# Ordering the third batch's first transforms nearer to their use in a fused Fourier mixer and channel mix kernel

## Chip, cores and metric

One core of one Trainium2 chip. The metric is the device time of one execution in microseconds (us); lower is better. A difference counts as faster or slower from 2% on, which is 12 us here.

## The reference, cut to what matters

```python
def _attn_ref(x, w_r, w_i, b_r, b_i):          # x: 8 x 3072 x 256
    X = np.fft.rfft(x, axis=1)
    Yr = Xr @ w_r - Xi @ w_i + b_r
    Yi = Xr @ w_i + Xi @ w_r + b_i
    # soft shrink of Yr and Yi by 0.01
    return np.fft.irfft(Y, n=x.shape[1], axis=1)

def _moe_ref(x, mu_k, mu_r, w_k, w_v, w_r):    # on the result of the first
    xk = mu_k * x + (1.0 - mu_k) * x_prev      # x_prev: one place earlier in the sequence
    xr = mu_r * x + (1.0 - mu_r) * x_prev
    k = np.maximum(xk @ w_k, 0.0)
    return 1.0 / (1.0 + np.exp(-(xr @ w_r))) * (k * k @ w_v)
```

## The kernel before

The transform of 3072 points is done as 96 by 32, in matmuls. Per batch there are: **first** transforms (eight units, line 280; the first two batches do this step another way), whose result A goes to DRAM (Adr) and comes back in another layout; **second** transforms (line 378 for the first group, line 395 for the rest), **mixing** with the complex weights (line 423), **back** transforms (line 462), whose result V goes through DRAM too (Vdr), and **last** inverse transforms (line 543) that write YT. Then each of the batch's six tiles of tokens has four **key** units (line 635), one **receptance** unit (line 662) and two **value** units (line 679).

The kernel text holds a small scheduler. Each unit has a due time and needs; among the units that are ready by the scheduler's own estimate, the one with the earliest due time is written next into the program. So the due times decide the order, once, when the program is built; on the chip each engine follows that order.

```python
    READ_US, WRITE_US = 7.0, 5.0

    def first(b, t0, t1):
                ...
                def store(k):
                    nc.sync.dma_start(out=Adr[b][:, 8 * q:8 * q + 8, :], in_=a)
                    done["a", b, q] = k + WRITE_US
                    n = 4 * b + q + 4
                    if 8 <= n < 4 * B:
                        load_x(n // 4, n % 4)
                        done["x", n // 4, n % 4] = k + 9.0
                    if q == 3:
                        at(k + WRITE_US, fetch)

                def fetch(k):
                    for hf in range(2):
                        A2[b, hf] = a2_pool.tile([128, NG // 2, D], BF16, name="A2")
                        for cj in range(4):
                            r0 = 24 * cj + 12 * hf
                            nc.sync.dma_start(out=A2[b, hf][32 * cj:32 * cj + 32],
                                              in_=Adr[b][r0:r0 + 12].rearrange("g n d -> n g d"))
                        for u in range(3 * hf, 3 * hf + 3):
                            done["A2", b, u] = k + READ_US * (1 + hf) / 2
            ...
            return Unit(t0 + (t1 - t0) * (2 * q + p) / 8, 0.44, needs, issue)   # due time first
    ...
    P = 71.5
    START = 50.0
    for b in range(B):
        s = START + P * (b - 1)
        ...
        else:
            fb += first(b, s - 0.9 * P, s - 0.2 * P)
            fa += middle(b, s, s + 0.5 * P)
            fc += last(b, s + 0.75 * P, s + 0.95 * P)
```

Batches count from 0 in the text, so `b == 2` is the third.

## Time and profile before

| | before |
|---|---|
| time, median of 3 | 595.51 us (595.29 to 595.68) |
| profiled span | 593.3 us |
| TensorE busy | 566.7 us, 96% |
| VectorE busy | 519.3 us, 88% |
| ScalarE busy | 425.5 us, 72% |
| third batch's last first-transform starts | 93.96 us |
| its A (first half) back | 110.4 us |
| its second transform starts | 120.91 us |

A kernel like this is read from its bound engine: where does TensorE stand still, and what was it waiting for? The prediction shows the lines. The column that names "idle before" in the groups, and the list of waits, give the answer per stretch of time.

### The profile page before, as it was taken

What the parts mean: (1) busy time and instruction counts of PE and PEld (TensorE: products, weight loads), DVE (VectorE), ACT (ScalarE), POOL (GpSimd) and SP (SyncE); (2) the same over time, 40 slices, a digit from 0 to 9 for tenths busy, and PEclk for the clock granted to TensorE, in tenths of its full rate; (3) what the DMA queues carried; (4) which work ended last, traced back from release to release, by engine and by line L of the source; (5) the groups of instructions that cost most, each with busy time, mean ns of one, the idle gap of its engine ahead of it and who ended that gap; (6) DMA issues with size and microseconds to landing.
All of it is one profiled execution on the core that took longest, in us unless ns stands there. A gap on an engine that the chain in (4) does not pass through costs nothing.

```text
span 593.3 us, 12315 instructions
## 1 busy us (share of the span) xinstructions
PE 566.7 (96%) x4824; PEld 428.9 (72%) x4891; DVE 519.3 (88%) x834; ACT 425.5 (72%) x467; POOL 23.5 (4%) x53
## 2 busy tenths in 40 slices
PE   4989999999999999999999999999999999999996
PEld 3878666777767787677777777677876787776665
DVE  7788999789998899888998989988999889979883
ACT  6887967677768677676777677777776867766652
POOL 7001000000000000000000000000000000000000
PEclk9999999999999999999999999999999999999999
DMA  8936888624599256773478655683338722362223
GB/s 150 167 80 158 186 193 226 178 72 104 129 225 237 60 139 140 204 225 67 116 167 245 154 120 129 165 238 106 100 93 235 178 55 73 103 164 72 68 57 90
DMA packets 68878, 84.06 MB, mean 142 GB/s; under 512 B 9042, under 2 KB 53844, under 8 KB 68820
## 3 DMA queue, kind: packets, MB, share of 16 engines
q1 hardware_dynamic: 62916, 68.98, 41.7%
q0 software_dynamic: 5712, 14.03, 15.1%
q8 instruction: 38, 0.62, 0.4%
q10 hardware_dynamic: 192, 0.26, 0.2%
q14 instruction: 20, 0.16, 0.1%
HBM read 50.07 MB, written 47.19 MB: 164 GB/s over the span
## 4 chain that ended last, share of the span: by engine, by line
PE 81%; ACT 7%; DVE 4%; DMA 3%; issue 2%; SPq 1%; POOL 0%; POOLq 0%; DVEq 0%; ACTq 0%
PE banks L679 27%; PE banks L635 23%; PE banks L423 14%; PE banks L662 5%; PE banks L462 3%; PE banks L280 3%; PE banks L395 3%; ACT rl L641 2%; PE banks L543 2%; ACT rg L667 1%; DMA xs<-in_x_dram 1%; DMA Adr<-A 1%; ACT YT L227 1%; PE banks L353 1%; SPq L305 1%
## 5 line engine op out<-in xcount | busy, mean ns | idle before, releaser
L641 ACT ACTIVATE rl<-banks 128x1024 bf16<-128x1024 f32 x192 | 193.5, 1028 | 94.0 <-PE banks L635 88.2
L635 PE MATMUL banks<-xk,wk 128*128 128x512 bf16 x701 | 188.7, 379 | 5.3 <-DVE xk L608 0.7
L679 PE MATMUL banks<-wv,k 128*128 128x256 bf16 x1536 | 183.0, 272 | 0.4 <-ACT rl L641 0.3
L679 PEld LDWEIGHTS <-k 128*128 128x128 bf16 x1536 | 149.3, 98 | 29.1 <-issue 1.4
L647 DVE TENSOR_TENSOR k<-rl 128x1024 bf16<-128x1024 bf16 x192 | 130.3, 684 | 13.3 <-ACT rl L641 13.3
L635 PEld LDWEIGHTS <-wk 128*128 128x128 bf16 x768 | 73.9, 98 | 60.7 <-issue 3.1
L423 PEld LDWEIGHTS <-XT 128*128 128x128 bf16 x768 | 74.5, 98 | 16.4 <-issue 0.9
L423 PE MATMUL banks<-wr,XT 128*128 128x256 bf16 x384 | 73.3, 272 | 0.6 <-ACT A L227 0.2
L423 PE MATMUL banks<-wi,XT 128*128 128x256 bf16 x384 | 73.3, 273 | 0.0
L608 DVE SCALAR_TENSOR_TENSOR xk<-diff,muk,YT 128x512 bf16<-128x512 bf16 x96 | 69.1, 744 | 0.2
L608 DVE SCALAR_TENSOR_TENSOR xr<-diff,mur,YT 128x512 bf16<-128x512 bf16 x96 | 68.7, 744 | 0.0
L690 DVE TENSOR_TENSOR o<-banks,rg 128x1024 f32<-128x1024 f32 (+1 forms) x49 | 58.6, 1196 | 3.7 <-PE banks L679 3.4
L227 ACT ACTIVATE YT<-banks 128x768 bf16<-128x768 f32 x59 | 44.9, 827 | 12.1 <-PE banks L543 9.1
L662 PE MATMUL banks<-wrm,xr 128*128 128x256 bf16 x384 | 49.8, 272 | 0.1
L227 ACT ACTIVATE XT<-banks 128x1024 bf16<-128x1024 f32 (+2 forms) x45 | 42.8, 956 | 9.2 <-PE banks L395 8.4
L667 ACT ACTIVATE rg<-banks 128x1024 bf16<-128x1024 f32 x48 | 49.1, 1024 | 0.0
L227 ACT ACTIVATE A<-banks 96x1024 bf16<-96x1024 f32 (+1 forms) x41 | 41.3, 1022 | 8.0 <-PE banks L280 6.2
L440 ACT ACTIVATE z<-banks 128x1024 bf16<-128x1024 f32 x32 | 32.7, 1022 | 19.9 <-PE banks L423 19.8
L662 PEld LDWEIGHTS <-xr 128*128 128x128 bf16 x384 | 37.2, 98 | 11.6 <-issue 0.2
L227 ACT ACTIVATE V<-banks 128x1024 bf16<-128x1024 f32 x35 | 35.9, 1024 | 11.6 <-PE banks L462 10.6
L602 DVE TENSOR_TENSOR diff<-YT 128x1024 bf16<-128x1024 bf16 x48 | 32.8, 683 | 3.8 <-ACT YT L227 3.8
L452 DVE TENSOR_TENSOR Y<-z,Y 128x1024 bf16<-128x1024 bf16 x48 | 33.2, 693 | 1.7
(101 smaller groups left out, 437.1 us busy)
## 6 DMA issues: line engine op xcount, KB each, us to landing
out_dram<-o SPq DMA_DIRECT2D x188, 128.0 KB, 2.3
xs<-in_x_dram POOLq DMA_DIRECT2D x32, 384.0 KB, 6.2
Vdr<-V SPq DMA_DIRECT2D x192, 64.0 KB, 1.8
V<-Vdr SPq DMA_DIRECT2D x32, 384.0 KB, 6.3
Adr<-A SPq DMA_DIRECT2D x24, 384.0 KB, 5.3
A<-Adr SPq DMA_DIRECT2D x48, 192.0 KB, 4.5
wk<-in_moe_w_k_dram POOLq DMA_DIRECT2D x1, 512.0 KB, 11.7
wv<-in_moe_w_v_dram POOLq DMA_DIRECT2D x1, 512.0 KB, 13.5
```

The source lines that it names most:

```text
L227: nc.scalar.activation(out, in_, AF.Copy, bias=0.0, scale=1.0)
L423: nc.tensor.matmul(o, lhs, w[:, c, :], start=(w is wr and c == 0), stop=(w is wi and c == NCD - 1))
L452: nc.vector.tensor_tensor(out=y, in0=z, in1=y, op=ALU.subtract)
L602: nc.vector.tensor_tensor(out=df, in0=y, in1=yp, op=ALU.subtract)
L608: nc.vector.scalar_tensor_tensor(out=m[:, c, :], in0=df[:, c, :], scalar=mu[:, c:c + 1], in1=yp[:, c, :], op0=ALU.mult, op1=ALU.add)
L635: nc.tensor.matmul(ps[:, 512 * f:512 * f + 512], wk[:, c, 128 * ff:128 * ff + 128], xk[:, c, :], start=(c == 0), stop=(c == NCD - 1))
L641: nc.scalar.activation(rl, ps, AF.Relu, bias=0.0, scale=1.0)
L647: nc.vector.tensor_tensor(out=k2, in0=rl, in1=rl, op=ALU.mult)
L662: nc.tensor.matmul(ps[:, 256 * q:256 * q + 256], xr[:, c, 128 * q:128 * q + 128], wrm[:, c, :], start=(c == 0), stop=(c == NCD - 1))
L667: nc.scalar.activation(rg, ps, AF.Sigmoid, bias=0.0, scale=1.0)
L679: nc.tensor.matmul(ps[:, 256 * q:256 * q + 256], K2[t][:, ff, 128 * q:128 * q + 128], wv[:, ff, :], start=(ff == 0), stop=(ff == NCF - 1))
L690: nc.vector.tensor_tensor(out=o[:, lo:hi], in0=ps[:, lo:hi], in1=rg[:, lo:hi], op=ALU.mult)
```

## The change

The due times of the third batch's first transforms start later (121.5 - 0.5 x 71.5 = 85.75 us instead of 57.15) and end later (114.35 instead of 107.2). The intent is to do them nearer to their use and to let the second batch's work go ahead of them.

```diff
-            fb += first(b, s - 0.9 * P, s - 0.2 * P)
+            fb += first(b, s - (0.5 if b == 2 else 0.9) * P, s - (0.1 if b == 2 else 0.2) * P)
```

The order on TensorE that comes of it differs in one stretch only. Here F is a first-transform unit of the third batch, L a last inverse unit of the second batch, K, R and V the token units, S0 and S second transforms of the third batch, M mixing (half a unit). Both rows begin with the sixth F.

```
before: F F F V K V K R K K L V K V K L R L L K V L K L L V K L K R K         S0 S K V S K M V M F K S R M M ...
after:  F L L V K V K R K F K L L V K V K R K F L K V L L K V L K R K K V     S0 S S K V F M M K S R M M ...
```

## The prediction

> **What bounds the kernel now.** I read the page first: shares of the span by engine, then the chain that ended last.
>
> ```profile
> span 593.3 us, 12315 instructions
> ...
> PE 566.7 (96%) x4824; PEld 428.9 (72%) x4891; DVE 519.3 (88%) x834; ACT 425.5 (72%) x467; POOL 23.5 (4%) x53
> ...
> PEclk9999999999999999999999999999999999999999
> ...
> PE 81%; ACT 7%; DVE 4%; DMA 3%; issue 2%; SPq 1%; POOL 0%; POOLq 0%; DVEq 0%; ACTq 0%
> ```
>
> TensorE is busy for 96% of the span at full granted clock, and 81% of the last-ending chain is its matmuls. It runs one fixed order of work, so what matters is TensorE time that is lost while the instruction at its head waits. A change that only reorders cannot shorten its 566.7 us; it can only remove or add idle time. So I asked next for the busy time of each engine in the stretches around the third batch's first transforms (columns: stretch and length, then busy time and instructions of each engine, clock, DMA share, GB/s):
>
> ```profile
> 80.00:93.09 13.09, 12.98 (x91) 8.95 (x91) 12.14 (x18) 8.04 (x9) 0.00 (x0) 1.00 0.83 232
> 93.09:102.33 9.24, 9.19 (x62) 6.19 (x62) 8.49 (x12) 6.61 (x8) 1.01 (x2) 1.00 0.99 223
> 102.33:120.90 18.57, 17.73 (x170) 13.38 (x172) 14.71 (x26) 12.70 (x16) 0.00 (x0) 1.00 0.57 147
> 120.90:131.00 10.10, 9.96 (x87) 7.63 (x87) 8.85 (x15) 6.87 (x8) 0.00 (x0) 1.00 0.25 65
> ```
>
> From 93.09 to 131.00 us TensorE loses 0.05 + 0.84 + 0.14 = 1.03 us. That is nearly all that a better order could win here. The waits of TensorE from 93 to 121 us name part of it:
>
> ```profile
> PE banks L635 <- DVE YT L563: 0.4, 1, 0.4
> PE banks L543 <- ACT YT L227: 0.2, 1, 0.2
> ```
>
> Both belong to the second batch's last inverse transforms (line 543) and the padding behind them, which in this order come in a bunch just before their result is needed.
>
> Last I read the DMA queue of SyncE in order of time, because the third batch's first transforms go out to DRAM (Adr) and come back in another layout (A) before the second transform (line 378, the first of its kind for the batch) may start:
>
> ```profile
> 95.05 1.57 SPq L291 DMA_DIRECT2D Adr<-A  x2
> ...
> 104.61 3.90 SPq L305 DMA_DIRECT2D A<-Adr  x8
> 108.61 5.33 SPq L701 DMA_DIRECT2D out_dram<-o  x8
> ```
>
> The second of the two stores is issued at 96.30 us, the fetch at 104.61 (8.3 us for a store's round), and the four DMAs of the first half land by 110.4. The second transform starts at 120.91: **about 10 us of slack**, with nothing waiting.
>
> **What the Trainium skill says.** "DMA: Bandwidth & Descriptors", section "Two DMAs through the same engine are not ordered": a DMA that reads what another wrote must wait at the issuing engine for the first one's completion. The trace agrees: the queue stands still from the store to the fetch, and the landing of the fetches is one more trip. The same page, section "Issuing engines are not separate DMA queues": transfers of all issuing engines share the same 16 DMA engines and interleave. The trace agrees: the line of stores to Adr shows landings of 2.9 us at least, 5.3 median and 8.9 at most, the longest where loads of x and V are in flight beside them. "TensorE: Matmul & The Clock Gate", section "Measured speedup vs the span model": matmuls start and end strictly in the program's order. So a late A would stop everything behind it on TensorE; the trace of before has no late A and cannot show it, but its matmuls stand in the listed order.
>
> **The change part by part.** It adds and removes no matmul: the listing of the order has the same 9784 TensorE rows, with the same counts of each kind. Only the due times of the third batch's eight first-transform units move, and the scheduler gives a new order only from about 93.5 us to about 128 us; after that all engines' orders are equal again. Three effects.
>
> (1) *Where the transforms land.* Before, units start at 71.53 (three), 76.11, 84.84 and 93.09 (three). In the new order the first six stay where they are; the seventh and eighth go behind inverse transforms and token units. I placed them by adding the measured pace of the units in the new order, from 93.09: a first-transform unit 0.43 us (two matmuls of 96x512), an inverse unit 0.34, a key unit 0.87 (four of 128x512), a receptance or mixing unit 0.87, a value unit 1.75 (sixteen of 128x256). This puts the seventh at 101.2 and **the eighth at 110.1 us**, and the second transform, which now comes behind one more key unit and one more value unit, at **122.3 us** if nothing waits. The same sum for the old order gives 119.7 where the trace has 120.9, and 128.2 for the first common unit where the trace has 129.6: so 1.4 us is what the old order loses here, somewhat more than the 1.03 that idle shows, because of short gaps.
>
> (2) *The round trip, now later by 17 us of which only 1.4 are given back.* From the last first-transform's start to the store's issue took 1.94 us in the fourth batch (172.44 to 174.38). The store then took until the fetch 8.9 us there, 7.4 in the fifth batch, 8.8 in the sixth, 6.4 in the seventh, 5.2 in the eighth, where no more x is loaded. Here one load of x goes out at the same moment (the buffer is released by the eighth unit), and one tile's output just before, but V's fetch has long landed by then (93.1 us). I choose 6.5, what the store issued at 78.90 took beside one load of x. The four fetches of the first half then took 5.8 us (104.61 to 110.44), I choose 5.7. Sum: 110.1 + 1.95 + 6.5 + 5.7 = 124.25 us, against 122.3 on TensorE. **The new wait is about 1.9 us**; with 5.2 for the store it is 0.6, with 8.9 it is 4.3.
>
> (3) *The inverse transforms come sooner and spread,* at 93.5 instead of 102.3. Their input V has landed at 93.05, just in time. The padding then is done long before the token mixing that reads it, so the two waits of 0.6 us should go, and perhaps 0.9 of the 1.4 us in all.
>
> On the path: +1.9 - 0.9 = **+1.0 us**, so 595.5 + 1.0 = 596.5 us. TensorE is the bound to the end, the order behind is unchanged, so nothing later gives the wait back.
>
> **Rivals.** *A, no new wait, small gain:* the store lands in 5 us and the fetch in 5, A is there at about 122.3, and the 1.4 us of the old order go: 594.1 to 594.8. For it: the DMA share falls from 0.99 to 0.57 after 102 us, so there is room. Against: a batch's last store never came back in less than 5.2 us, and that was without a load of x beside it. *B, the round trip is as slow as in the fourth and sixth batch* (8.8 to 8.9): a wait of 4.3 us, 598 to 599. Against: there V's 1.5 MB were in flight beside the store, here they are not. *C, the held queue delays outputs:* SyncE stands from the store to the fetch, outputs queue behind, and the gating on VectorE runs out of its two output buffers. In the old order the same stand of 8 us cost no such wait, and tiles come 12 us apart; I give it under 1 us. *D, an earlier inverse transform waits for V:* margin only 0.5 us, but nothing before 93 us changes, so I expect none. None reaches 2%, which is 12 us.
>
> **Range and chances.** The store's 5.2 to 8.9 us gives a wait of 0.6 to 4.3, less 0.5 to 1.4 of old idle: from -0.8 to +3.8, with the middle at +1.0. Runs before spread by 0.4 us. I take 594.6 to 598.9, and 98% for within 2%.
>
> **What would show it.** Right: in the changed trace a wait of TensorE (or its weight load) for a DMA of A at the first line-378 matmul near 122 to 125 us, the last store to Adr issued near 112, the fetch near 118.5; no wait on the padding (line 563); busy TensorE time equal, its idle larger by about 1 us. Wrong: no wait at line 378, or a longer stand of the queue; outputs (line 690) waiting for their buffers; or a different time far from this stretch, which the equal order does not lead me to expect.

## The result and the profile after

| | before | after |
|---|---|---|
| time, median of 4 each | 595.4 us (594.63 to 595.68) | 594.8 us (593.86 to 594.91) |
| profiled span | 593.3 us | 593.1 us |
| third batch's last first-transform starts | 93.96 us | 110.72 us |
| its second transform starts | 120.91 us | 123.73 us |
| its fifth mixing unit starts | 148.46 us | 148.44 us |

The ratio is 0.9988 with a 95% interval of 0.9971 to 1.0006: the same.

The stretches of the changed kernel, in the same columns as those of the kernel before in the prediction:

```profile
93.09:102.33 9.24, 9.04 (x74) 6.48 (x74) 8.93 (x18) 6.21 (x8) 0.51 (x1) 1.00 0.76 199
102.33:120.90 18.57, 18.35 (x162) 13.39 (x163) 16.11 (x23) 13.82 (x17) 0.51 (x1) 1.00 0.54 127
120.90:131.00 10.10, 9.45 (x85) 7.28 (x84) 7.72 (x12) 6.20 (x8) 0.00 (x0) 1.00 0.81 185
```

The middle stretch lost 0.84 us of TensorE time before and loses 0.22 now; the last lost 0.14 and loses 0.65. The sum over the three is 1.03 before and 1.07 now. Part of this is matmul records that are missing: in before_again, which has all of them, the same three stretches lose 0.00, 0.62 and 0.08 us, 0.70 in all, and the 0.62 are just the two waits. The one large wait of TensorE that is left there, from the list of its waits between 93 and 131 us:

```profile
PE banks L378 <- DMA A<-Adr: 0.6, 1, 0.6
```

The two waits of before (at line 635 for the padding of line 563, and at line 543) are no longer in that list. SyncE's queue and TensorE in order of time show how the new wait comes about (start, length, engine, line, what; a bracket gives the idle time ahead and what ended it):

```profile
110.72 0.60 PE L280 MATMUL banks<-xs,FT 96*96 96x512 bf16 x2
...
112.64 0.31 SPq L291 DMA_DIRECT2D Adr<-A  x1
117.66 3.90 SPq L305 DMA_DIRECT2D A<-Adr  x8
...
123.73 0.38 PE L378 MATMUL banks<-G,A 128*128 128x256 f16 x2 [0.60 <-DMA A<-Adr]
```

The eighth first-transform starts at 110.72; its store is issued at 112.64; the fetch follows at 117.66, 5.0 us later; the four fetches of the first half land by 123.60 by their semaphores, and TensorE goes on at 123.73. So the trade of the prediction took place in the trace, and in this profile it came out even: 0.6 us of waits gone, 0.6 us of a new wait.

### The profile page after: what moved, and what is told of

The parts are those of the page before. It is cut to its first block, busy times and chain, and to the rows that moved or that the text cites. A ratio compares the mean times of both kernels' runs of the same rounds, so it can differ in the third digit from the quotient of the medians.

```text
span 593.1 us, 12318 instructions
## 1 busy us (share of the span) xinstructions
PE 566.7 (96%) x4825; PEld 428.9 (72%) x4891; DVE 519.8 (88%) x833; ACT 425.1 (72%) x467; POOL 24.0 (4%) x53
## 4 chain that ended last, share of the span: by engine, by line
PE 81%; ACT 7%; DVE 4%; DMA 4%; issue 2%; POOL 1%; SPq 0%; DVEq 0%; POOLq 0%; ACTq 0%
PE banks L679 27%; PE banks L635 23%; PE banks L423 14%; PE banks L662 5%; PE banks L462 3%; PE banks L395 3%; PE banks L280 3%; ACT rl L641 3%; PE banks L543 2%; ACT rg L667 1%; DMA V<-Vdr 1%; ACT A L227 1%; DMA Adr<-A 1%; ACT YT L227 1%; DMA A<-Adr 1%
```

## The experiments

Times of whole runs spread by up to 4 us on some chips, more than the effect. So each run is also read from its trace over one fixed piece of work: from the start of the sixth first-transform of the third batch (93.09 us before; up to there all orders are equal) to the start of that batch's fifth mixing unit (148.46 us before; from about 133 us on all orders are equal again). This **stretch** leaves out the run's start and what comes later. In the kernel before it was 55.37 us, in a second profile of it 55.37, and in a third build with one load moved 55.36. It repeats to 0.01 us when no transfer is waited for.

Theory 1: the new order wins about 0.6 us (x_late below puts it at 0.8) by the inverse transforms being sooner and spread, and loses the wait for A, one for one. Rivals: the gain lies elsewhere; the wait is absorbed; or the first runs' 0.9988 is a real gain.

| run | wait for A | store to fetch | clock 0.5 after it | stretch | median, ratio to before (95%) |
|---|---|---|---|---|---|
| before | none | 8.3 (of two) | no | 55.37 | 595.4 |
| before_again | none | 8.4 (of two) | no | 55.37 | 594.1, one run |
| after | 0.60 | 5.0 | no | 55.32 | 594.8, 0.9988 (0.9971 to 1.0006) |
| after_again | 1.08 | 5.3 | no | 55.80 | 595.32, 1.0004 (0.9981 to 1.0027) |
| after_third | 1.88 | 6.3 | no | 56.59 | 595.82, 1.001 (0.9987 to 1.0034) |
| s0_later | 1.05 | 6.8 | no | 55.70 | 594.3, 0.9992 (0.9968 to 1.0016) |
| s0_earlier | 3.13 | 5.1 | 3.41 us | 59.91 | 602.19, 1.0109 (1.0074 to 1.0144) |
| s0_earlier_2 | 2.71 | 5.0 | no | 57.81 | 600.17, one run |
| s0_one_value | 4.43 | 6.8 | 3.41 us (once more later) | 60.56 | 598.2, 1.0032 (1.0 to 1.0065) |
| ends_earlier | none | 5.1 | no | 55.18 | 596.14, 1.0019 (0.9995 to 1.0043) |
| x_late | none | 3.3 | no | 54.56 | 593.61, 0.9973 (0.9957 to 0.999) |
| x_late_2 | none | 3.1 | no (once later) | 54.56 | 594.05, 0.9986 (0.9961 to 1.0011) |
| before_x_late | none | 5.3 (of two) | no | 55.36 | 595.06, 0.9995 (0.9975 to 1.0014) |

All columns but the last are of the profiled run; that of s0_one_value was slow, and its ratio leaves it out. All outputs were correct.

### The changed kernel again (after_again, after_third)

No edit.

> The changed kernel unaltered, in five rounds, with a second profile. Theory 1 (the change is a wash: a wait of 0.6 us at the third batch's second transform takes the place of some 0.6 us of waits behind the inverse transforms): ratio to the kernel before 0.9995 to 1.0005, the wait of TensorE for A at line 378 again 0.4 to 0.9 us, and the first mixing matmul after 148 us at the same time as before within 0.1 us. Rival (the first four runs' 0.9988 is a real gain of 0.7 us, made outside this stretch): ratio 0.998 to 0.999, and the profile must show where.

> The changed kernel a third time, as the neighbour of the run with the load held back. Theory 1: wait for A at line 378 of 0.5 to 1.5 us, ratio to the kernel before 0.9985 to 1.0015. Rival: no wait, or a ratio outside this.

Ratios 1.0004 and 1.001: with 0.9988 the three lie on both sides of 1, so the first call's 0.7 us is no gain that holds. The wait for A came each time, but with 0.60, 1.08 and 1.88 us it is not a constant. It is longer than the 0.4 to 0.9 us expected of after_again and than the 0.5 to 1.5 us expected of after_third, and the stretch of after_again was not at the old time within 0.1 us but 0.43 us longer: these expectations missed. What varies is the round of the store to Adr: 5.0, 5.3 and 6.3 us. Why it varies stays open.

The three profiles show best that the wait is lost one for one. The stretch less the wait is 55.32 - 0.60 = 54.72, 55.80 - 1.08 = 54.72 and 56.59 - 1.88 = 54.71 us: all that differs between them is the wait.

### The second transform sooner (s0_earlier, s0_earlier_2)

```diff
-                            done["A2", b, u] = k + READ_US * (1 + hf) / 2
+                            done["A2", b, u] = k + READ_US * (1 + hf) / 2 + (-2.0 if b == 2 else 0.0)
```

The scheduler believes that A is back sooner, so the order becomes `... L K R K S0 S V K S K M V M F K S R M M ...`; the transforms before it stay.

> The changed kernel, but its scheduler is told that the third batch's A is back 2 us sooner, so the second transform is ordered one key unit and one value unit (2.6 us of work) sooner while the transforms before it stay. Theory 1 (TensorE stands in order for A, and time lost there is lost for good): A lands as before near 123.6 us, the wait grows from 0.6 to about 3.2 us, and the time rises by 2.6 us over the changed kernel: about 597.4 us, ratio 1.004 to the kernel before. Rival (slack behind the wait takes it up): ratio 1.000 to 1.001 in spite of a longer wait.

> The kernel of the run with the 3.1 us wait, profiled again. If the halved clock behind that wait is a consequence of the idle time, it comes again or not by where a free-running window falls: with it the mixing after 148 us is some 4.5 us late, without it 2.6 to 3.2 us.

The wait grew to 3.13 and 2.71 us as expected, so nothing absorbed it. But the loss was larger than the wait in the first of the two. The stretches of that run around the wait, in the columns as above (clock third from the right):

```profile
121.78:125.19 3.41, 1.26 (x15) 1.20 (x16) 0.85 (x2) 0.18 (x1) 0.00 (x0) 1.00 1.17 237
125.19:128.60 3.41, 3.41 (x15) 1.98 (x14) 2.08 (x4) 0.00 (x0) 0.00 (x0) 0.50 0.56 178
```

For 3.41 us behind the wait TensorE was granted half its clock, which by half of 3.41 costs about 1.7 us of work. With a wait of 2.71 us the second run had no such stretch. That fits: the two runs have the same order, and without the wait for A their stretches are 59.91 - 3.13 = 56.78 and 57.81 - 2.71 = 55.10 us, 1.68 apart. This order also makes another wait of 0.27 us, for an eviction of A (line 227), in both. The second run's 600.17 us is more than its stretch explains: its trace has 2.0 us of waiting for V near 327 us, which has nothing to do with the edit. The four timed runs went from 598.24 to 603.56; what the three that were not profiled lost is not known.

### One value unit behind instead of before (s0_one_value)

The same edit with -0.6 in place of -2.0. One value unit moves from before S0 to behind S; nothing else moves.

> The changed kernel with one value unit (sixteen matmuls, 1.75 us) moved from before the third batch's second transform to behind it; nothing else moves. Theory 1 (time that TensorE loses at the wait is lost for good, one for one): the wait grows from 0.6 to 1.1 us to 2.3 to 2.9 us, and the first mixing matmul after 148 us comes 1.75 us later than in the changed kernel, at 150.2 us plus what the start of the run is later. Rival (the 3.1 us wait of the run before cost more than itself because the clock was then halved): if this wait also is long enough for the clock gate, a stretch of clock 0.5 follows and the loss is 3 us or more; if the clock stays at 1.0, the loss is 1.75 us.

The wait was 4.43 us, more than expected, since the store's round took 6.8 us this time; and the halved clock came again, from 125.93 for 3.41 us, as the rival had it. So theory 1's number could not be read cleanly. The stretch less the wait is 60.56 - 4.43 = 56.13 us, 1.41 more than the 54.72 of the changed kernel; the halved clock can account for about (3.41 - 0.35) / 2 = 1.5 of it, since the wait covered its first 0.35 us. The sum roughly holds, the 1.75 us were not seen by themselves. The runs went from 594.71 to 604.1.

### The second transform later (s0_later)

The same edit with +2.0: one more key unit before S0.

> The changed kernel, but its scheduler is told that the third batch's A is back 2 us later, so one more key unit (0.87 us) stands before the second transform; the mixing units behind it bunch up. Theory 1: no wait at line 378 (A lands near 123.6, the transform is due near 124.0), 0.6 us less than the changed kernel: near 594.2 us, ratio 0.999, unless the bunched mixing makes a new wait. Rival (the wait only shows another limit): the wait is gone, but the mixing units after 148 us are not earlier.

The wait did not go: the store's round took 6.8 us, and A came later than the 0.87 us that the extra unit gives. The expectation missed; that the median, 594.3, is near the expected 594.2 is chance. The run shows that 0.9 us of room is less than what the round trip itself varies by.

### Half of the change (ends_earlier)

The edit is to the kernel before; the due times of the third batch's first transforms start later, as in the change, and keep their old end.

```diff
-            fb += first(b, s - 0.9 * P, s - 0.2 * P)
+            fb += first(b, s - (0.5 if b == 2 else 0.9) * P, s - (0.2 if b == 2 else 0.2) * P)
```

The order becomes `F F L V K V K R K K F L V K V K R L L K L K V L L K V L K R K S0 ...`.

> Only one half of the change: the third batch's first transforms get the later start of their due times (0.5) but keep the old end (0.2). The seventh stays near 93.5 us, the eighth moves to about 101.8 instead of 110.7; the inverse transforms of the second batch start at about 94 instead of 102.3. Theory 1 (gain and loss come from two separable parts): A is back near 115, no wait at line 378, and no waits behind lines 543 and 563, so 0.6 us less than either kernel: mixing after 148 us is 0.5 to 0.8 us earlier, ratio about 0.999. Rival (the inverse transforms being sooner brings nothing by itself): ratio 1.000 and mixing at the old time.

The eighth starts at 103.1 us, A is back in time, and the old waits at lines 543 and 563 are gone. But the list of TensorE's waits from 93 to 140 us has two others:

```profile
PE banks L635 <- ACT rg L667: 0.4, 1, 0.4
PE banks L662 <- ACT A L227: 0.3, 1, 0.3
```

So this order wins 0.19 us of stretch (55.18 against 55.37), not the 0.6 expected. The two old waits, 0.6 us, did go; the two new ones, 0.7 us, took most of that back. Both wait for ScalarE. So having the inverse transforms sooner is not worth 0.6 us in every order. The timing (1.0019, interval to both sides of 1) decides nothing.

### The load beside the store held back (x_late, x_late_2, before_x_late)

At the moment of the store (112.64 us) a load of x for the fifth batch goes out, because the eighth unit frees its buffer (111.61 us). The edit makes GpSimd first read one element per row of the third batch's A, so that the load goes out only when A has landed. It is not needed before about 198 us.

```diff
-                    n = 4 * b + q + 4
+                    n = 4 * b + q + 4; (b, q) == (3, 0) and nc.gpsimd.tensor_copy(out=n1c[0:96], in_=A2[2, 1][0:96, 0, 0:1])
```

> The changed kernel, but the load of x that goes out at the same moment as the third batch's last store (near 111.6 us) is held back until that batch's A has landed. Theory 1 (the load beside it makes the store's round 5.0 to 6.8 us): the store comes back in 3 to 4 us, A's first half lands at or before 122.5 us, no wait at line 378, mixing after 148 us 0.6 us earlier than in the changed kernel. Rival (store and fetch take their time by themselves): store 5 us again, wait 0.6 to 1.1 us.

> The changed kernel with the load of x held back, again, beside the changed kernel itself on the same chip. Theory 1 (the wait for A is the whole price of the change, and the load beside the store makes it): no wait at line 378 again, ratio to the kernel before 0.997 to 0.9995, and 0.6 to 1.1 us below the changed kernel. Rival (the first three rounds' 0.9973 was chance): ratio 0.9995 to 1.0005.

> The kernel before with the same load of x held back until the third batch's A has landed. Theory 1 (holding the load helps only where TensorE waits for A): the old order has 10 us of slack there, so the store comes back sooner but nothing is won: ratio 0.9995 to 1.0005, the two waits of 0.2 and 0.4 us near 110 us stay. Rival (the load costs time of itself, through the shared transfers): ratio below 0.999 here too.

The queue and TensorE in x_late:

```profile
110.98 0.60 PE L280 MATMUL banks<-xs,FT 96*96 96x512 bf16 x2
...
112.90 0.31 SPq L291 DMA_DIRECT2D Adr<-A  x1
116.15 3.91 SPq L305 DMA_DIRECT2D A<-Adr  x8
...
123.23 0.38 PE L378 MATMUL banks<-G,A 128*128 128x256 f16 x2
```

The store comes back after 3.25 us instead of 5.0 to 6.8, A's first half has landed at 122.1, and the second transform starts without a wait (there is no bracket). The stretch is 54.56 us in both profiles: 0.81 us less than the kernel before, and 0.76, 1.24 and 2.03 less than the changed kernel's three profiles. So this order is worth 0.81 us, and the wait ate it. The two old waits named above make 0.62 of the 0.81; the rest was not taken apart. In the kernel before, the same edit also brings the round down, from 8.3 to 5.3 us for its two stores, and wins nothing (55.36): there the round trip has slack. That tells theory 1 from the rival that the load costs time of itself.

x_late is the best of the versions tried: 0.9973 and 0.9986 of the kernel before. The first interval lies below 1, the second does not. It is 0.8 to 1.6 us in 595, far from the 2% that would count. Beside it on the same chip the changed kernel (after_third) had a median 1.8 us higher, more than the 0.6 to 1.1 expected, as its wait was 1.88 us in the profile.

The profiled run of x_late_2 took 597.74 us, the slowest of its six, and shows why single runs spread. Near 251 us it waits twice for V, and then:

```profile
250.18:253.59 3.41, 1.76 (x17) 0.88 (x14) 2.35 (x4) 2.11 (x3) 0.00 (x0) 1.00 1.03 281
253.59:257.00 3.41, 3.10 (x28) 2.68 (x29) 1.19 (x7) 2.21 (x3) 0.00 (x0) 0.50 0.55 216
```

Two waits of 1.13 and 0.77 us, of which the first stretch holds all but the end (3.41 - 1.76 = 1.65 us not busy), were followed by a halved clock. But the busy time does not decide it alone. In after_third a stretch of the same length with less of it was followed by full clock:

```profile
122.27:125.68 3.41, 1.53 (x16) 1.17 (x15) 3.41 (x6) 0.66 (x1) 0.00 (x0) 1.00 1.12 227
125.68:129.10 3.42, 3.42 (x36) 2.75 (x34) 0.86 (x3) 3.13 (x4) 0.00 (x0) 1.00 0.84 235
```

The edges are comparable: where a trace has several changes of the granted clock, they lie whole multiples of 3.413 us apart (in s0_earlier 125.19, 128.60 and 596.23 us), and 122.27 us lies 138 such steps before the one change in after_third, at 593.31 us. What decides stays open.

### The kernel before again (before_again)

No edit.

> The kernel before, profiled a second time. Both theories: the waits behind the inverse transforms (0.2 us at line 543 and 0.4 us at line 635 near 110 us) come again, since they follow from the order alone; no wait at line 378; what differs between two profiles of the same kernel is the start (to 78 us) and the wait for V near 251 us.

As expected: the waits of 0.4 and 0.2 us came again, to the tenth of a microsecond, and the stretch was the same. The wait for V near 251 us was 1.3 us in the first profile, and in the second no wait for V was there. That difference alone is larger than what the change does to this kernel's time (-0.05 to +1.22 us of stretch).

## Why the prediction was right, and where it was off

The measured 594.8 us lies in the range of 594.6 to 598.9, near its low end, and "within 2%" was right. That it lies inside is in part luck: it is 0.2 us above the lower end, one of the four runs (593.86) is below it, and the wait of that profile was the smallest of the three. By its steps:

1. **TensorE is the bound and the change moves only idle time: right.** Its busy time is 566.7 us in both profiles (570.7 and 570.8 where no record is missing). But the 1.03 us of lost TensorE time that the prediction read is partly missing records: with all of them it is 0.70.
2. **Where the eighth unit lands, 110.1 us: right to 0.6 us** (110.72). The due date of the second transform, 122.3, was early by 0.8 (123.13, which is 123.73 less the wait): adding the pace of units leaves out the short gaps between them. The prediction had seen this in the old order (119.7 against 120.9), but did not carry it over to the new one. Both dates shifted by about the same, so the wait was hardly touched.
3. **The round trip: right in kind, over-sized for the first profile.** The wait for A at line 378 came, in all seven profiles in which the eighth unit was late and the load beside it was there. Its size was put at 1.9 us; it was 0.60, 1.08 and 1.88 in three profiles of the changed kernel. The mis-sized term is the store's round: 6.5 us chosen, 5.0, 5.3 and 6.3 measured. The fetch, put at 5.7, took 5.9 to the first half's landing in the first profile.
4. **The gain of 0.9 us from the new order: right,** 0.81 in x_late. The reason that the prediction gave for it, that the two waits of 0.6 us go, holds for most of it. What it left out is that another order can make new waits: ends_earlier loses the same two and wins only 0.19.
5. **The net of +1.0 us: this is the step that failed,** by the wait's size. By the stretch the net is -0.05, +0.43 and +1.22 us in three profiles, so about +0.5 on average; by the timed ratios it is not to be told from nothing. The range does not follow from its own terms either: 595.5 with -0.8 to +3.8 is 594.7 to 599.3, not 594.6 to 598.9. And the round trip moved by 16.1 us (93.96 to 110.1), not 17; no sum uses this. The 9784 rows are of a listing; a full trace has 4891 matmuls and 4891 weight loads.
6. **"Nothing later gives the wait back": not tested cleanly.** The wait for V near 251 us differs between profiles of one kernel (1.3 and none before; 1.67, 0.97 and 0.22 after), so anything carried past it is drowned. Left open: why that transfer varies.

Rivals: A (small gain) describes the first profile's net best, though the wait came; B (a store as slow as 8.8 us) did not come, the longest was 6.8; C (outputs held) and D (waiting for V at 93.5 us) did not appear in the list of TensorE's waits. The statement that matmuls start and end in program order stands in the section "The mechanism" of "TensorE: Matmul & The Clock Gate". The runs agree with the statement: everything behind the waiting matmul of line 378 was late by the wait.

## What to carry to other kernels

Before moving a producer nearer to its use, take the slack of the round trip behind it from the trace and compare it with what that trip varies by, not with its median: here some 10 us were cut to nothing, and the trip varied by 1.8 us. Look at what the move releases at the same instant, since a load whose buffer comes free with the last store runs beside that store; here the reordering won its 0.8 us only with that load held back. And when the effect is below the spread of whole runs, measure a fixed piece of work in the traces: it repeated to 0.01 us where the runs differed by 4 us.

## What the Trainium skill lacked or had wrong

- "TensorE: Matmul & The Clock Gate", section "HAM oscillation — how this bites in real kernels", gives as the rule that idle gaps of TensorE must not exceed about 3.4 us. Here a single wait of 3.13 us, and two waits of 1.13 and 0.77 us, were followed by 3.41 us at half clock; a wait of 2.71 us was not. That the halved stretch is one such window long agrees with its section "What's actually happening". So the length of one gap does not decide alone; nor does TensorE's busy time in the 3.41 us before, since 1.76 us of it (x_late_2) were followed by half clock and 1.53 us (after_third) by full clock.
- "DMA: Bandwidth & Descriptors", section "Issuing engines are not separate DMA queues", says that transfers of all engines interleave, but gives no size for it. Here one store of 384 KB took 3.1 to 3.3 us from issue to the dependent fetch without a load of x beside it, and 5.0 to 6.8 us beside one of 384 KB issued 1 us ahead.
- No page says how much the same transfer varies from run to run in one kernel: the wait for V near 251 us was between nothing and 1.9 us.
